# Eighteen weight sums on GpSimd instead of VectorE, a planner that counts instruction packets, and three held tiles released one by one

## The chip, the cores and the metric

One NeuronCore of a Trainium2 chip runs the whole program. Its engines work side by side, each through its own list of instructions in order: TensorE (PE; its weight loads are listed apart as PEld), VectorE (DVE), ScalarE (ACT), GpSimd (POOL) and SyncE (SP), which here only issues DMAs. They wait for each other through semaphores. The metric is the device time of one execution in microseconds, the median over the runs shown.

## The reference

Two steps, one behind the other, in float32 (the weights come as 64-bit floats, and the kernel turns them into 32-bit ones itself):

```python
# delta rule: 4 batches x 8 heads, 768 steps, head dimension 48
k_n = k / (norm(k) + 1e-6)
for t in range(768):
    y[t] = q[t] @ state
    state = state + beta[t] * outer(k_n[t], v[t] - k_n[t] @ state)
# then, on x = y as (3072 tokens, 384): RMS norm and a gated feed-forward network
xn = x / sqrt(mean(x*x) + 1e-6) * rms_g
out = (silu(xn @ w_gate) * (xn @ w_val)) @ w_out      # 384 -> 1536 -> 384
```

## The kernel before

The 768 steps are cut into 12 chunks of 64. Within a chunk the recurrence is a triangular system: products of keys (`scores`, `invert`), an inversion in small steps on VectorE (lines 709 to 807 for chunks 0 and 1, lines 869 to 930 for the later ones, with a round trip through DRAM), products with values and state (`recur`), the update of the state. Each chunk gives 256 tokens, on which the feed-forward network runs: for chunks 0 and 1 plainly (`ffn_plain`, up-products L1331, down-products L1313), for chunks 2 to 11 with fewer products by sums of factors (`ffn`, L1426, and `down`, L1483). So PE has two kinds of work: long streams of 128-row products, and bursts of small products (64 instructions or more in about 1 us) that carry the recurrence.

Every piece of work is an operation of a `Plan`: engine, estimated duration, what it reads and writes. The order of all 2790 operations is written out in the string `ORDER`. The text of the kernel does not search for it; it was found beforehand. At build time `Plan.times` walks this order and works out a start for each operation; from these starts follow which PSUM bank each result gets (there are eight) and where PE gets filler matmuls on an identity matrix (L1594), which go to a bank of their own and keep PE busy while the first chunk is prepared. `Plan.run` then emits the instructions. `OVERLAP`, `BEGIN`, `FETCH` and the like are constants of that estimate. In the version before, the supply of PE with instructions is estimated as a backlog that is filled by work and drained at a rate (`FETCH`, `AHEAD`).

The weights come in 18 pieces of 128 partitions by 768 values of 64 bits (`weights`). For each piece: one DMA of 768 KB into one of seven `raw` places, two ACT operations (L475 and L476) that take the upper and the lower 32-bit words, one DVE shift (L470), and one sum of the two words (L473) into `w_in` or `wo_sb`, from where the feed-forward network reads them. The seven `raw` places lie in tiles that are used otherwise later: three in `more`, two in `hf`, two in `wsum`. The first four pieces are loaded at once. The next three places are held back by `hold` (L493): a one-column POOL copy from `u_` into each place, so that the DMA of the piece has to wait for chunk 0's `u_`.

Names that return below: `norms` (L584 to L612) makes 1/norm(k) with a POOL power (L589, L608); `invert` and its steps L776 (transpose), L782 and L801 (small products), L795 and L807; `pt` (L633); `mr0` (L1134) and the L1114 products give u and y of a chunk; L1214, L1220 and L1221 make the RMS factor `rs`, the last two on POOL; L1232, L1236 and L1241 scale `yn` with it, L1259 transposes `yn` for the feed-forward network. L819 scales the keys on POOL. L1052 is the first product with the state.

Two functions carry the part that differs:

```python
P.add("DVE", 0.57, shifted, pr, w=cak)              # L470
P.add("DVE", 0.97, added, pr, r=cvk + cak, w=done)   # L473
def hold():
    for n in range(HELD, 7):
        t = raw[n].bitcast(FP32)[:, 0:1]
        P.add("POOL", 0.15, ..., 29, r=[("u", 0, 0)], w=[("raw", n)])
```

Of the kernel before, what the change touches and what calls it, by code (L numbers as in the profile page):

```python
# [9 lines left out]
FP32 = mybir.dt.float32  # L10
# [6 lines left out]
C = 64  # L17
W = 32
# [3 lines left out]
FETCH, AHEAD = 67.0, 120.0  # L22
EARLY, FETCH0, AHEAD0 = 130.0, 50.0, 150.0
# [9 lines left out]
    "#.#'#&#3#)#4###,#-#(#/#*#0#T#C#`#W#>#^#a#_#w#U#X#k#Y#$#Z#d#l#b#n#m#o#c#H#t#V#e#+#u#f#[#]#q#v#x#s#R#y#S#@#z#M#p#{#1#|"  # L33
    "#?#2#}#E#i#~#j$C$#${$$#r$'$($%$&$)$*#N$D$/#J$.#D$+$0$1$,$H#I%$$E#=$2$F$-%)#K$7$5#L$3$8$6$<#O#h#A$=$>$;$4$9#P$G$?%V$:"
    "#g$I$B#F$L$K$J$i$l$O$N$M#B$P$Q$R&2%Y$[$S$@#G$T$]%W%Z$^$V$k$j$U$_$v%X$f$q%e$`$a$W$m$b$Y%[$c$d#Q$X$Z$e$n$o&Q$A&E%]%`%^"
    "$|&F$p%a$~$w&I%_&G%b$x&H&J$y$s%3%c$r&M%d$g%.&K$t&N$h&3&L$z#5&R&O%f$}$u'2%g%+&4&P%h'3%%%#&S'4&+%i%&&,&T%j%*%=%k&X%8%l"
    "&U%/%B%,&Y&V(4%1%m(5&^%n&Z%0#8&_&-#7&[%q%G%r%o%2&W%4%s%p&]&`%x%5%6%y%L&.#:%t%z%C#<&/&a%{%u%7&0%v%-%D'-%w%}%~%|%'%(&c"
    "&#&1%:#%&5&d'Q%H'0%9&b&?%E%?%Q%F'T'a%J'R&''.%I'1&&&@%K&$&('S&7%;&)'U&%#6'/%>'V&*&e%@'5%A'W'X%<'8%R'Y&h':'[%T%S&f'Z'9"
    "(6&i']%U&8'7%M&6&m'6&j(7%N&g(8'^)-#9).(<'K(9&k):#;';);%O&r'<%P'_&s&9'=)/'?&n)0'>(:'L&l)n'M&o&t&p'b&u&q'@'`'N)q'A'c)o"
    "'B&:&w'P)r'd'e)p'O'f'C&v'g'h'G'i)s'j&x&A)u'k*P'H&|&C&y'l'D'E'F)t&{'m'I'J)y&z&})w'n&B)v'o'$&~*Q'#)x'p'%&D'q(;(I'r's'&"  # L40
    "'t)<(E){'*'''u(=(J'v(Q(F(K)1'w'x(>(G'y(H)K)2'z(L)z)=(M(C(?)>(N(@)L('(R()(O)}'{(P)?(%(W)~(*)M(+)|(X(,((*#($(S(A*$(D*%"
    "(T(&*&'~*''((Y(U*((#'}(V(-'|*)(Z)N&;(.***W(/*X*+(](2'+*,(1')(0)O(^(3*-)P)Q([*.(_&<)R*/(B*R(c(`)S(a(d*0*S(h(e*T*1)T*2"
    "*U*3&=*4(i(f*5)U)m(m*6(j(k(n)@*:*V*9)V(r,9*Y*8)X*7)W(s-$(o)Y(p*^)3,<(t,:)G(w,;)[*G)H(x,=*H*B)l*C,>)4*<(u*=)I+s*>,@*F"
    ",?(|)5)Z,C(y+u,B)A(},D)6,A(z*I)7*@)a*D)B(b*E)b)C,K*?)D*A)])c)E,L(g,F*;)^)_,E)d(l)`*J-#)e+t)f*K)8(q)g*M-+)9*L*O)h(~*`"
    "*Z)i*N)j',)#)k+y)F*[,G(v+z,H,I,J,M-%({,N+{,O,P,Q*b,R-&*d,S*c-',T)$*e,U-(,V)%,W)&,X*f)',Y*h)(*g*_)*-)+0,Z)+*j))*i.i-*"
    "*n*k),+2*o.j*p,[*t,]+v*u*q*l,^*v.l*r.k,_*z*a*w+w*s*x*{+4*m*y,`.m+3+(,a+x+5+8,b+$+),c+**|+%.n,d+<++*}+1,e+,*]*~+=+6,f"
    ")J+|,h,g+7,i+-+9.o+D+.+&+:+>+'+#+/,k+B+},t+~+_,s+?,$,r-,+C/V+@+E,8+F-2.p+H,m+G,l,#+J,w+I,v,%+N,7,j+K,n.q+O,q+L,p+A.H"
    "+P,u.r+Q.s+;+R+M,'+Z.w.~+V.v+S,&.t,,+T+W,x.u,-+U.E,o,y/U+X,z.G,(.F,|+a+Y.x,)+],.,/.y+g,},*&>,++`+[-0.I+e,~,0,{+^/^.J"
    ",1,2/#.K+h--,3,4,5+c,6/W.z+f.{.|.}/$/X+k/%/&+b/'/(-.+d/)-/-4/*+l-1/Y/+-6-5+n/,+m+i/Z-7/-.M/.-://-8+j/0-<-9/1+o/[/2-@"
    "-;1?+p-=+r-_+q-A->-B/31@-3-F-C-H/4-G-D-a-?-I/51B-L1A-c/]-M-J-E/6-b-V-d/71C-K-N-W-g/8-X-Y-R/9-`-O-k/:1D.L-e-S/;-l.N-T"  # L50
    "-P-f/>-U-h/<-Z1E.O/=.P-s-Q/?.R-[-m.Q-]-q.S-t-n/J.1/F1F.U/I.T-i.V-o-^-u.h/H-r-p/K/_1G-v/L/M.g-w1H-j1I-y.W-x1T1L-}.-1J"
    ".%1K-~1M/N.#.X.&.)/E-z2,.$0x-{.*.'/O-|1O/`.(.Y...2.+1N/P.,/D.3.//T/B.0/S0z/G1U/b/C/Q.9.7/R.Z.4/A/@.5.8.:2-/c0y1P/a1Q"
    ".=.61R.[1S1V1W.]1X.^0~1Y._1Z.>1[.@0{1]/e1#.`.?.;.a2..b.c.d.e.f2//g/f20/i.<1^1_/k21/j1`/h.A0|1a/l1b/m.B1c1$.D/o.C22/n"
    "/s3r/p/u/t/q/y/r3s/v/{3t1d/z/d/}/|1e0#/~1f0}3u1%/w230$1g240-1&1'053v1h1)4_0)1(0.071i1*0/0900/x1,1j3w060%1+0*0;0:1-1k"
    "084`0A1l0<0=1m0B3x0+010&1n0>0'0C1.021o0I0D031q0?0G0,1p1>0J040K1/0(0H3y1r0O0L0E1=0M0P1~3z1y0N0Q1{0R0S25103{3|0W3}3N0X"
    "3~0T4$260Y4#0Z0U0F4+2#0[0@1}0`2$0d0]110V1|0^4,1v0_0f3P4%0a1u1z0b0l1t2%1s0c0j1x122&1w0e4&0g1328142;152'3O160h172(182*"
    "192)1:2+0m0k3T1;0i1<274'0n3U4(4)4*4a4-4.0p4/40414b42430o2=0q4c440r2?450s4d2<2A462@470t2B2>48492C0u0v2I4e0w2D2E4g6H2J"
    "292h2F2j4:6I6J2O4;2K2P4<2Q2L6K2U4=2R4f2M3Q2G2N2V2S3R2H4>2`2T6L4?2k2l2:2a2[4@2b2m2p2c3S4A3V2W6M4B2i2t2X4C2n2]2Y4D2^3W"
# [18 lines left out]
    "?->o>m?/>p>n@0?)?.@1@2?%?*?3@4@3?+?1?0?4@5?2?,?9@6@7?=?:@8?E@9?>?5@:???;?@?G?6@<?F?A?&@;?I?H@=?B?7?K?<?J?C?M?L?Q?N?S"
    "?D@>?R?W?8?T?Y?X?[@??^?]?Z?d?U?_?O@@?`?e?h?f?a?l?g?b?i@A?t?V?j?c?k?m?P?v?n?p?u?o?r?q?z?w?s@B?x@C?}@D?{@E@F@G@$@H?y?|"
    "@I@J@K?~@%@L@&@'@M@#@O@N@Q@P@S@R@U@T@(@V@Y@)@*@`@Z@+@[@a@b@]@f@^@c@x@W@g@d@X@p@e@z@q@l@_@r@{@s@|@m@yA$@}@~@tA#A(A%@u"
    "A*A)@v@hA+A.A,@i@nA2@w@j@oA/@kA0A&A-A3A4A1A:A5A6A;A>A7ABA8A?A<AJA9A@A'A=AAACALAFADAKAEAHAGAOAMAIATANARAQAPAVASAUAXAW"  # L80
    "A]A^A_AYAZA["
# [34 lines left out]
class Plan:  # L116
# [38 lines left out]
    def times(self, order, banks, until):  # L155
# [8 lines left out]
        server, self.end, mode, backlog, lands = 0.0, 0.0, 0, 0.0, []  # L164
        for op in order:
# [41 lines left out]
    def run(self, free, filler=None, until=0.0):  # L207
# [24 lines left out]
def kernel(  # L232
# [209 lines left out]
    def weights(first, last):  # L442
# [14 lines left out]
        for n, (dst, src, keys) in list(enumerate(todo))[first:last]:  # L457
# [14 lines left out]
            def added(dst=dst.bitcast(U32), top=tiled(top), rest=tiled(rest)):  # L472
                nc.vector.tensor_tensor(out=dst, in0=top, in1=rest, op=ALU.add)  # L473
# [1156 lines left out]
```

## Time and profile before

| | |
|---|---|
| Median of 3 runs | 668.11 us (666.66, 668.11, 669.87) |
| The profiled execution | 668.94 us, of which 667.2 us from the first instruction to the last |
| PE busy, PEld busy | 654.4 us (98%), 604.8 us (91%) |
| DVE busy | 543.3 us (81%) |
| ACT, POOL busy | 295.7 us (44%), 133.7 us (20%) |
| PE instructions | 9934 matmuls and as many weight loads |
| DMA moved | 69.36 MB, 104 GB/s on average |

A busy PE in such a profile is not a PE without losses, as a matmul's span covers its whole passage. The chain of waits is of more use: it starts from the last instruction and goes back from each step to what released it. In it "issue" is time in which an engine waited for nothing that the profile shows. The windows view gives, for each engine in a stretch, busy time and in brackets the number of instructions; the timeline gives start, duration, engine, line, operation, tiles, shape and count, and at the end the idle time before it with what ended it.

### The profile page before, as it was taken

To read this page: it belongs to the slowest core of one execution; us is meant where nothing else is said; L and a number is where in the kernel's file an instruction comes from. 1 tells how busy PE (TensorE), PEld (TensorE's weight loads), DVE (VectorE), ACT (ScalarE), POOL (GpSimd) and SP (SyncE) were. 2 spreads that over 40 slices of the span, in tenths; PEclk is the share of its full clock that TensorE was granted. 3 is DMA by queue.
4 is the path that set the end of the run, shared out by engine and by line. 5 is a ranking of instruction groups with operands and counts; after the bars stand their busy time and mean duration, and the time that the engine had idled before them with its cause. 6 is when DMAs were issued, how large, how long until landed. Compare 5 with 4: busy or idle time off the path is not lost.

```text
span 667.2 us, 23209 instructions
## 1 busy us (share of the span) xinstructions
PE 654.4 (98%) x9934; PEld 604.8 (91%) x9934; DVE 543.3 (81%) x1147; ACT 295.7 (44%) x705; POOL 133.7 (20%) x204
## 2 busy tenths in 40 slices
PE   9999999999999999999999999999999999999997
PEld 5687887887799999999999999999999999999997
DVE  5879799888898798799888898799898799557463
ACT  4677553235336435454445345344445244263240
POOL 2210423021610410520410410420410301000000
PEclk9999899999999999999999999999999999999999
DMA  9959754666465566376375565666355333300101
GB/s 213 239 157 269 203 140 72 109 160 103 64 113 78 118 106 127 68 136 102 68 126 98 88 113 108 111 114 114 73 98 103 74 63 67 63 31 20 25 1 25
DMA packets 270423, 69.36 MB, mean 104 GB/s; under 512 B 257456, under 2 KB 262576, under 8 KB 270000
## 3 DMA queue, kind: packets, MB, share of 16 engines
q1 hardware_dynamic: 269280, 67.68, 51.1%
q8 instruction: 78, 1.28, 0.8%
q10 hardware_dynamic: 1040, 0.20, 0.2%
q14 instruction: 25, 0.20, 0.1%
HBM read 49.76 MB, written 22.02 MB: 108 GB/s over the span
## 4 chain that ended last, share of the span: by engine, by line
PE 91%; DVE 3%; issue 2%; POOL 2%; SPq 1%; DMA 1%; ACT 0%; POOLq 0%; ACTq 0%
PE bank L1426 40%; PE bank L1483 19%; PE bank L1331 8%; PE bank L1313 4%; PE bank L563 3%; PE bank L1037 3%; PE bank L1594 3%; PE bank L1114 2%; PE bank L1100 1%; PE bank L782 1%; PE bank L801 1%; PE bank L1171 1%; PE bank L979 1%; PE bank L999 1%; SPq L377 1%
## 5 line engine op out<-in xcount | busy, mean ns | idle before, releaser
L1426 PE MATMUL bank<-xf,w_in 128*128 128x128 f32 x1440 | 178.8, 276 | 0.3 <-DVE tmp L1436 0.3
L1426 PEld LDWEIGHTS bank<-xf,w_in 128*128 128x128 f32 x1440 | 169.3, 192 | 1.8 <-DVE tmp L1436 0.5
L1436 DVE TENSOR_TENSOR tmp<-tmp,bank 128x512 f32<-128x512 f32 x180 | 120.1, 682 | 46.9 <-PE bank L1426 28.9
L1426 PE MATMUL bank<-xf,more 128*128 128x128 f32 x960 | 122.8, 276 | 0.1
L1426 PEld LDWEIGHTS bank<-xf,more 128*128 128x128 f32 x960 | 114.9, 192 | 1.3 <-DVE tmp L1436 0.3
L1438 ACT COPY tmp<-bank 128x512 f32<-128x512 f32 x120 | 68.5, 587 | 99.9 <-PE bank L1426 78.5
L930 DVE TENSOR_REDUCE acc<-acc 128x30 f32<-128x90 f32 (+4 forms) x150 | 71.0, 473 | 5.2
L1442 ACT ACTIVATE tmp<-tmp 128x256 f32<-128x256 f32 x120 | 47.6, 415 | 61.9 <-DVE tmp L1436 61.8
L1483 PE MATMUL bank<-wo_sb,hf 128*128 128x192 f32 x360 | 64.0, 329 | 0.0
L1483 PEld LDWEIGHTS bank<-wo_sb,hf 128*128 128x128 f32 x360 | 58.0, 190 | 1.1 <-issue 0.4
L924 DVE TENSOR_TENSOR acc<-acc,at 128x60 f32<-128x60 f32 (+4 forms) x150 | 52.9, 353 | 5.9 <-POOL at L904 2.8
L1443 DVE TENSOR_TENSOR hf<-tmp 128x256 f32<-128x256 f32 x120 | 47.7, 418 | 3.0 <-ACT tmp L1442 2.2
L608 POOL TENSOR_TENSOR knrm<-ksum,half 128x16 f32<-128x16 f32 x11 | 32.0, 2913 | 85.2 <-DVE ksum L587 85.1
L869 POOL TENSOR_TENSOR at<-at,beta_b 128x256 f32<-128x256 f32 (+3 forms) x32 | 18.0, 593 | 149.0 <-DMA at<-dkk 149.0
L1313 PE MATMUL bank<-wo_sb,hf 128*128 128x384 f32 x96 | 33.8, 488 | 1.1 <-issue 1.1
L1331 PE MATMUL bank<-xp,w_in 128*128 128x256 f32 x144 | 34.7, 397 | 0.1
L1331 PE MATMUL bank<-xf,w_in 128*128 128x256 f32 x144 | 33.0, 382 | 0.0
L1331 PEld LDWEIGHTS bank<-xp,w_in 128*128 128x128 f32 x144 | 28.0, 198 | 4.5 <-DVE hf L1340 0.2
L1283 DVE TENSOR_TENSOR xf<-xf 128x256 f32<-128x256 f32 (+1 forms) x70 | 27.5, 432 | 5.2 <-ACT xf L1253 2.6
L1331 PEld LDWEIGHTS bank<-xf,w_in 128*128 128x128 f32 x144 | 26.9, 190 | 4.5
L950 POOL COPY acc<-acc 128x128 f32<-128x128 f32 x40 | 16.3, 438 | 71.4 <-DVE acc L930 70.7
L1313 PEld LDWEIGHTS bank<-wo_sb,hf 128*128 128x128 f32 x96 | 17.8, 190 | 10.3 <-issue 1.3
(207 smaller groups left out, 989.4 us busy)
## 6 DMA issues: line engine op xcount, KB each, us to landing
at<-dkk SPq DMA_DIRECT2D x20, 256.0 KB, 4.3
vt<-in_v_dram SPq DMA_DIRECT2D x24, 192.0 KB, 4.4
out_dram<-tmp SPq DMA_DIRECT2D x48, 96.0 KB, 2.2
k<-in_k_dram SPq DMA_DIRECT2D x23, 192.0 KB, 4.7
dks<-k SPq DMA_DIRECT2D x14, 256.0 KB, 4.0
kt<-dks SPq DMA_DIRECT2D x28, 128.0 KB, 3.8
more<-in_moe_w_gate_dram SPq DMA_DIRECT2D x4, 768.0 KB
more<-in_moe_w_out_dram SPq DMA_DIRECT2D x4, 768.0 KB
```

The costliest lines, as they stand in the source:

```text
L608: P.add("POOL", 2.95, lambda: nc.gpsimd.tensor_tensor(out=knrm[i2], in0=ksum[i2], in1=half, op=ALU.pow), pn, r=[("ksum", i2), "half"], w=[ ...
L924: nc.vector.tensor_tensor(out=acc[:, 1:3, 0:n, j + 2 : W].rearrange("p a i t -> p i a t"), in0=acc[:, old, 0:n, j : j + 2, None].to_broadc ...
L930: nc.vector.tensor_reduce(out=acc[:, new, 0:n, j + 2 : W], in_=acc[:, lo : lo + 3, 0:n, j + 2 : W].rearrange("p a i t -> p i t a"), axis=A ...
L1283: P.add("DVE", V(128 * n), lambda dst=dst, a=a, b_=b_, op=op: nc.vector.tensor_tensor(out=dst, in0=a, in1=b_, op=op), pxv, r=[("xp", 0), ( ...
L1313: nc.tensor.matmul(po[p].t[:, 0:DM], hf[:, spot(f), 128 * p : 128 * p + 128], wo_sb[:, spot(f)], start=(f == f0), stop=(f == f1 - 1), skip ...
L1331: nc.tensor.matmul(ps.t[:, TOK * side : TOK * side + TOK], w_in[:, side, h_, 3 * t + i_, n : n + 128], x_[:, 2 * t : 2 * t + 2].rearrange( ...
L1426: nc.tensor.matmul(g.t[:, 128 * z : 128 * z + 128], fac[:, side, 128 * f : 128 * f + 128], xf[:, xs], start=(begin and z == 0), stop=False ...
L1436: P.add("DVE", V(512), lambda t=t, g=g: nc.vector.tensor_tensor(out=t, in0=t, in1=g.t, op=ALU.add), -1, r=[g], w=[tk], last=g)
L1438: P.add("ACT", A(512), lambda t=t, g=g: nc.scalar.copy(t, g.t), -1, r=[g], w=[tk], last=g)
L1442: P.add("ACT", A(256), lambda t=t: nc.scalar.activation(out=t[:, 0:256], in_=t[:, 0:256], func=ACTF.Silu), -1, w=[tk])
L1443: P.add("DVE", V(256), lambda t=t, f0=f0, p=p: nc.vector.tensor_tensor(out=hf[:, spot(f0) : spot(f0) + 2, 128 * p : 128 * p + 128], in0=t[ ...
L1483: nc.tensor.matmul(g.t[:, 0:192], a_[:, f], b_[:, f], start=(begin and f == 0), stop=(f == 5), skip_group_check=True)
```

## The change

```diff
-FETCH, AHEAD = 67.0, 120.0
-EARLY, FETCH0, AHEAD0 = 130.0, 50.0, 150.0
+PACKET = (130.2, 254.45, 314.0)
+LAG = (4.2, 0.55, 7.0)
...
 ORDER = (
...
 # Plan.times
+        first, each, reach = PACKET
+        count, asked, used, there, pe = 0, 0, 0, {}, 0.0
+        lag = lambda t: LAG[0] + LAG[1] * min(max(server - t, 0.0), LAG[2])
...
-                rate, store = (FETCH, AHEAD) if s > EARLY else (FETCH0, AHEAD0)
-                fill = 6.0 if s < until else 0.0
-                backlog = max(0.0, backlog - (rate - fill) * (s - at["PE"])) + op.size - rate * op.dur
-                late = max(0.0, backlog - store) / rate
-                backlog, end = max(0.0, backlog - rate * late), end + late
+                op.fill = []
+                if s < until and any(x == SPARE and s < SPARE or x <= pe for x in free):
+                    op.fill = fillers(pe, s)
+                pe = s + op.dur
+                count += 4 * len(op.fill)
+                while first + each * asked <= count:
+                    there[asked] = s + lag(s)
+                    asked += 1
+                more, late, long = count + op.size, 0.0, end - s
+                while True:
+                    a, b = first + each * asked, first + each * used + reach
+                    if a >= more and b >= more:
+                        break
+                    if a <= b:
+                        t = s + late + (long * (a - count) / op.size if op.size else 0.0)
+                        there[asked] = t + lag(t)
+                        asked += 1
+                    else:
+                        t = s + late + (long * (b - count) / op.size if b > count else 0.0)
+                        if used < asked and there[used] > t:
+                            late += there[used] - t
+                        used += 1
+                count, end = more, end + late
...
 # weights
             def added(dst=dst.bitcast(U32), top=tiled(top), rest=tiled(rest)):
-                nc.vector.tensor_tensor(out=dst, in0=top, in1=rest, op=ALU.add)
+                nc.gpsimd.tensor_tensor(out=dst, in0=top, in1=rest, op=ALU.add)
...
-            P.add("DVE", 0.97, added, pr, r=cvk + cak, w=done)
+            P.add("POOL", 1.55, added, pr, r=cvk + cak, w=done)
...
     def hold():
-        for n in range(HELD, 7):
-            t = raw[n].bitcast(FP32)[:, 0:1]
-            P.add("POOL", 0.15, lambda t=t: nc.gpsimd.tensor_copy(out=t, in_=u_[:, 0, 0:1]), 29, r=[("u", 0, 0)], w=[("raw", n)])
+        for n, t, key in ((HELD, u_[:, 0], ("u", 0, 0)), (HELD + 1, ms[0][:, 0], ("ms", 0, 0)), (HELD + 2, xp1[:, 0], ("x1", 0))):
+            out_, in_ = raw[n].bitcast(FP32)[:, 0:1], t[:, 0:1]
+            P.add("POOL", 0.15, lambda out_=out_, in_=in_: nc.gpsimd.tensor_copy(out=out_, in_=in_), 29, r=[key], w=[("raw", n)])
```

There are three parts and a consequence. The 18 sums (L473 before, L494 after) move from DVE to POOL. `Plan.times` counts PE's instructions: it takes it that they come in packets of 254.45, that a packet is asked for at instruction 130.2 and then every 254.45, is needed 314 instructions after that, and is there 4.2 us after the request plus up to 3.85 us more by the load of the DMA queue. The three held places are released one after the other: by chunk 0's `u_`, by its mean square `ms`, and by its normalised and transposed rows `xp1`. The consequence is a new `ORDER`: all 2790 operations are the same but for the engine of the sums, and 333 of the 580 PE operations stand at another place in PE's list than before; the lists of the other engines and of the DMAs differ as well. PE's filler matmuls go from 26 to 24 instructions. Line numbers behind line 200 rise by 21.

More of the change, by code (lines that the diff above doesn't have):

```diff
@@ L37 @@
[L37 to L46, printed above, removed]
@@ L77 @@
[L77 to L81, printed above, removed]
+    "#.#'#-#w###4#(#)#*#3#0#/#>#`#W#C#^#a#T#_#,#k#X#&#Y#Z#b#l#d#n#m#o#e#t#U#H#c#V#1#u#f#+#[#]#r#v#x#q#y#s#z#j#p#{#S#|#D#i"
@@ new lines @@
+    "#}#R#I#~#M$#$$$%$&$'$(#$$)$*#E#g$/#J$+%$$.$C#2$,$1#K#?$0$D#L$2#N$-$6#@$3$E$5$F$;$7${#A#h#=$<$8#F#P$9$>$H#O$=$:$?$G%V"
+    "$I$B$L$K$J$4$i#G$l$O$N$M$P$Q$R%Y$[$S$f$T$]%Z$^$j$V$_$q$U$W#B%)$`$a%W$X$Y$b%X$@$d$c#Q$Z%[$e$m$n$k%e&Q$v&E%]&3$o%^%`$r"
+    "&F$p$s&I%a%_%.&G$t$g&2&J%b$A#5&H$h$u%c%%&R$w%d$x&M%f%&%3$y'2&K#;%g%*%=%h&N$|&L$z#%&S&O%+$~&P&T'3%i$}&+%j&W&,&U%#'4%B"
+    "&V&X%8%k%0#<&Y%,%/%l%G%1&^%m&-%n%2&_&Z&[%r%-&]&.%5%p&4%'%4%o&/%x&`%(%y%L%C(4&c%z&0#6%q%:%6#:%E%9&d%s%>%Q&a%t&e%7%{%u"
+    "&6%v%D%|&1&&%H&''Q%w'-%F%~'.'0'R%J%I&b%}&#%@(<&(&5%K'a'T(5&)'U#7'S'/&$#8&*%?#9'1'V&7&%&f%A'8'W'X'5%;%S%<'Y&h%R'6']'["
@@ new lines @@
+    "(6)-&m'Z%T%N(;%U'7&i':(7'b'9'O%M&g).'^&j&8(8):'K)/(9%O';)0&k&l'<'_&n%P&r&o(:&9'M)n&p&q'='L'>'P&s'`'?'@'c&w&t&?'d&u)o"
+    "&@&:'e&x'f)p'B'g)q'h'G&|'H'i&y'A'I'j&}'J)r'k&C)K*P'l)s'm&v)u&z)t'n'C&~&{)y'o'D'E&A'F)x'p'$*Q'q)v'%)w'r&B'#(E's&D't(F"
+    ")1'u){'&'v(G(H(I'N);'*'y)<'w(J)2'x(='z(M(K)z)M)L(N(L)=(*)>(>'|(O''(&(S'{(@)}(,(+(P(?(T(C)3('(()|(X(U(#)~'((V(Q(Y',*#"
+    "()(%(R*$($(Z*%'~*&(A(^*'*X*((-'}*))N(.**(/(B([(W&;*+(0(1*W(3*,)O(_(D(2*-)Q(`(a(c*.*/*R(d)S*0&<(h)R*S(i*T*1(]*2(j*U)P"
+    "*3(e)T(f*4)4*5)?(m)U*6(k-$(n*V*9)m,9(r*Y*7(o*8(p(s*:)l)V)G,:(t,<,;(w(u,=*D)5)W*=)H(x*<)X*E)Y*G,>*H*@)Z+s*C,?*;,@(|+u"
@@ L82 @@
+    "?y@K@L?|@M@%@'@O@&?~@P@N@Q@#@S@R@U@T@(@V@Y@)@+@`@Z@*@[@a@W@b@]@f@^@c@d@g@x@e@p@l@q@z@_@r@m@|@s@{@X@y@t@}@~@uA$@vA#@n"
+    "A(@w@oA%A*A)@hA+A.@iA2@jA,@kA/A0A-A3A4A&A1A:A5A6A;A>A<A7ABA8A?AJA'A@A9AAA=ACALADAKAEAFAGAOAHAIATANAMAPARAQAVASAUAXAW"
+    "A]A_A^AYAZA["
 )
@@ L163, in times @@
                 g.taken, g.uses = False, g.left
-        server, self.end, mode, backlog, lands = 0.0, 0.0, 0, 0.0, []
+        server, self.end, mode, lands = 0.0, 0.0, 0, []
+        first, each, reach = PACKET
+        count, asked, used, there, pe = 0, 0, 0, {}, 0.0
+        lag = lambda t: LAG[0] + LAG[1] * min(max(server - t, 0.0), LAG[2])
         for op in order:
@@ L216, in run @@
                 spare = [x for x in free if x[0] == SPARE and s < SPARE or x[0] <= pe]
-                if s < until and spare:
-                    filler(fillers(pe, s), spare[-1][1])
+                if op.fill:
+                    filler(op.fill, spare[-1][1])
                 pe = s + op.dur
```

69 lines of the change are left out of this document (35 added, 34 removed).

## The prediction

> **What bounds the kernel now.** I read the page first, then the chain of waits, then windows and timelines where the chain leaves PE's stream.
>
> ```profile
> PE 654.4 (98%) x9934; PEld 604.8 (91%) x9934; DVE 543.3 (81%) x1147; ACT 295.7 (44%) x705; POOL 133.7 (20%) x204
> ...
> q8 instruction: 78, 1.28, 0.8%
> ...
> PE 91%; DVE 3%; issue 2%; POOL 2%; SPq 1%; DMA 1%; ACT 0%; POOLq 0%; ACTq 0%
> ```
>
> PE bounds the kernel, and 91% of the chain is its own matmuls, which the change leaves alone. Only 9% of 667.2 us, some 60 us, can be argued about, a part of it before PE's first feed-forward matmul. The chain there and behind it (start, us, what):
>
> ```profile
> 13.58 1.09 PE bank L563 x64
> ...
> 28.33 0.81 PE bank L782 x26
> 29.14 0.63 issue
> ...
> 30.77 1.05 PE bank L782 x32
> ...
> 32.45 1.99 PE bank L801 x64
> ...
> 37.57 0.86 DVE w_in L473
> ...
> 43.40 0.93 issue
> ...
> 44.60 7.98 PE bank L1331 x36
> ...
> 71.08 1.31 issue
> ...
> 73.87 4.43 PE bank L1331 x12
> ...
> 122.86 2.79 PE bank L1331 x12
> ...
> 171.18 1.06 issue
> ```
>
> Two things cost time. A weight sum (L473) is itself a link of the chain at 37.57. And PE stops four times here for 0.63 to 1.31 us with nothing to wait for. The windows view, from the start to these stops and to one of 0.9 us at 265.4 (L999, below), counts the instructions that PE had begun (in brackets, PE and PEld):
>
> ```profile
> 0.00:29.20 29.20, 27.72 (x350) 18.24 (x350) 20.76 (x64) 16.18 (x40) 6.19 (x11) 1.00 0.93 218
> 0.00:43.40 43.40, 40.62 (x731) 29.65 (x731) 29.73 (x86) 23.79 (x62) 11.59 (x19) 1.00 0.82 208
> 0.00:71.30 71.30, 67.28 (x1113) 52.03 (x1114) 55.89 (x146) 44.22 (x98) 14.50 (x20) 1.00 0.84 213
> 0.00:171.25 171.25, 165.39 (x2636) 131.17 (x2637) 143.27 (x323) 87.68 (x202) 39.22 (x47) 0.99 0.72 167
> 0.00:265.40 265.40, 258.55 (x4165) 219.58 (x4165) 223.80 (x491) 129.51 (x301) 62.28 (x84) 0.99 0.65 142
> ```
>
> The sums are 700, 1462, 2227, 5273 and 8330. From the first they are 3.0, 6.0, 18.0 and 30.0 steps of 254.5. PE's 19868 instructions over 78 packets of the instruction queue give 254.7. So PE stops where a packet of its own instructions is not there yet. The new planner's constants put these places at 444.2 + 254.45 k: 698.7 for k = 1, as measured.
>
> The Trainium skill speaks against that reading. "Runtime: NRT & Kernel Launch", section Instruction fetch mechanics, says that instructions come in 16 KiB blocks of 256, which fits the packets here, but also that the fetch is mostly hidden since instructions are issued more slowly than they are filled in. The second half doesn't hold in this trace, which has stops of up to 1.31 us; by it the sum below would be 2.1 us and not 7.1.
>
> **The change part by part.** *Sums off DVE.* DVE loses 18 instructions of 0.95 us (six of them in the first row below, the others at 946 to 960 ns), 17.2 us between 28 and 96 us. POOL gains 18. The trace has no integer sum on POOL; the nearest row is L819, two inputs of 768 elements, 1.48 us, so 26.6 us in all. A bound above is twice that row, 2.95 us, if integers cost it more; below is L1062's rate, 0.84 us for 384 elements, which gives 1.68 for 768 and so no gain over L819.
>
> ```profile
> L473 DVE CUSTOM_DVE_ANT_0 w_in<-xf,tmp x6: 948/954/1076, 28.7 to 85.3; 128x1536 uint16<-128x1536 uint16 x6
> L819 POOL TENSOR_TENSOR k<-k,krec 128x768 f32<-128x768 f32 x11 | 16.2, 1477 | 31.8 <-issue 14.3 <-DVE krec L612 11.0 <-PE bank L1331 4.5
> L1062 POOL TENSOR_TENSOR r<-r,bt x2: 836/836/837, 76.3 to 79.0; 128x384 f32<-128x384 f32 x2
> 28.72 0.95 DVE L473 CUSTOM_DVE_ANT_0 w_in<-xf,tmp 128x1536 uint16<-128x1536 uint16 x1
> 29.59 0.44 DVE L776 STREAM_TRANSPOSE x2bd<-mt 128x256 f32<-128x256 f32 x1
> 29.95 0.65 DVE L633 TENSOR_TENSOR pt<-bank,mask_p 128x512 f32<-128x512 f32 x1
> 30.70 1.01 PEld L782 LDWEIGHTS bank<-mt,m1bd 64*64 64x64 f32 x32 [0.17 <-DVE pt L633]
> 20.00:40.00 20.00, 18.91 (x419) 15.58 (x417) 16.40 (x40) 10.73 (x29) 5.98 (x7) 1.00 0.74 191
> 40.00:60.00 20.00, 18.71 (x320) 15.98 (x320) 16.78 (x41) 16.45 (x31) 1.17 (x4) 1.00 0.81 213
> 60.00:80.00 20.00, 18.69 (x273) 15.44 (x272) 17.51 (x38) 12.46 (x20) 7.39 (x6) 0.91 0.86 240
> 80.00:100.00 20.00, 19.89 (x405) 16.82 (x404) 17.59 (x33) 10.95 (x26) 4.76 (x3) 1.00 0.60 163
> ```
>
> Off the chain this buys nothing: from 45 us on PE has its stream. On the chain it counts twice. At 28.72 a sum stands ahead of the transpose L776 and of `pt` L633, for whose bank PE's second L782 block waits until 30.70: 0.95. At 37.57 it is a link: 0.86. Together -1.8 us. The bounds are 0 (the power on POOL or the L801 products take over) and -3.1 (the whole detour from 28.33 to 32.45 but for one L782 block of 1.05, since the new list puts the q transposes L540 ahead of both L782 blocks). I take -1.8, as both pieces are seen. On POOL a wait is added: each sum waits for ACT and the shift, and behind it in POOL's list stand the power, the key scaling L819 and `rs`. In the new list one sum stands ahead of chunk 0's first `rs`, between it and the release by `u_`, and the next two stand behind the second `rs`. So `rs` is cleared unless that one sum is late.
>
> One sentence of the skill on the price: "GPSIMD Engine Reference", section 3.1, has a two-input sum of 2048 elements at 4497 ns, by which 768 would take an estimated 1.69 us and POOL's load would be 3.8 us more, off the chain but for one sum of 0.2.
>
> *Packets.* I walked both built lists of PE with the cadences of the rows (64 products of 64 columns 1.09, 32 of L782 1.05, 12 of L1331 2.79) and looked at the 314 instructions ahead of each packet's place. In the old list they last under 5.5 us at 10 places, in the new one at 3; behind the first feed-forward matmul at 8 and at 1. At 71.08 the stretch grows from 4.4 to 7.2 us, at 43.40 from 4.6 to 6.1, at 265.4 from 3.7 to 6.3. At 29.14 it stays (5.7 and 5.8), at 171.18 it doesn't grow (6.9 and 6.3), and the place between 29 and 43 with 4.9 us falls to 4.0.
> - Before 45 us: 0.93 goes, up to 0.9 may come at the shortened place; -0.5, bounds +0.9 and -1.56 (both stops).
> - 71.08: -1.31. Behind it PE ran at half clock for some 3.6 us (granted 0.91 in 60:80, so 20 x 0.09 / 0.5): 12 matmuls of L1331 took 4.43 instead of 2.79. That goes with the stop: -1.64. If the stop stays, both stay.
> - 171.18: 0, bounds -1.06 and +0.6.
> - Behind 180 us, the waits of PEld:
>
> ```profile
> PEld bank L999 <- issue: 2.1, 5, 0.9
> PEld bank L1483 <- issue: 1.2, 6, 0.2
> ...
> PEld bank L1100 <- issue: 0.7, 3, 0.2
> PEld bank L979 <- issue: 0.5, 2, 0.2
> 103.08 0.62 PE L1259 MATMUL bank<-ident,yn 128*128 128x128 f32 x3 [0.57 <-ACT yn L1241]
> ```
>
> L1483's six of 0.2 look like a change of shape and stay. Of L999, L1100 and L979 (3.3 together) and what stretches without an idle row I take -2.0, bounds 0 and -4.0.
>
> *The three releases and the new DMA order.* The third held piece now waits for chunk 0's transposed rows, and on SP a load into `more`, which went out at 27.41, stands behind two releases.
>
> ```profile
> 27.41 1.31 SPq L377 DMA_DIRECT2D more<-in_moe_w_gate_dram  x1
> ...
> 39.95 0.57 SPq L377 DMA_DIRECT2D wsum<-in_moe_w_val_dram  x1
> ```
>
> That load feeds the second half of the network, which PE's list reaches after all up-products of the first, and the last release comes about when the old `wsum` load went out, so I take 0. If that cover is gone, the third piece's columns wait: one down- and two up-products (some 1.3 and 2.79) are 4 us of other work on PE, beyond which each us counts.
>
> *Other places.* At 103.08 PE waits 0.57 for `yn`, behind POOL; -0.3, bounds -0.57 and +1.6. A list packed more tightly meets small delays that were in gaps before: +0.5, bound +5.
>
> Sum: -1.8 -0.5 -1.31 -1.64 -2.0 -0.3 +0.5 = -7.05. The profiled execution took 668.94, so 661.9; the median lies 0.83 below it: 661.1, called 661.0.
>
> **The rivals.**
> 1. *The stops don't go*: the DMA load, not the spacing, decides when a packet lands, and the new list has stops at other places. For: 171.18 stopped with a 6.9 us stretch. Left are the sums (-1.8) and 103.08 (-0.3): 668.11 - 2.1 = 666.0. The skill's rule that fetches are hidden gives the same time. Against: five stops at whole packets.
> 2. *POOL and DVE get in each other's way* (slower). The one mechanism: a POOL sum holds off a DVE instruction with two SBUF inputs, or the reverse. For:
>
> ```profile
> 99.29 1.33 DVE L869 TENSOR_TENSOR at<-at,beta_b 128x1024 f32<-128x1024 f32 x1
> L1220 POOL TENSOR_SCALAR ms<-ms x11: 218/222/1082, 99.6 to 593.9; 128x2 f32<-128x2 f32 x11
> ```
>
> A 222 ns step took 1082 while L869 ran. Six sums stand on POOL beside chunk 1's inversion. If all 18 block fully, DVE gains 17.2 and loses 26.6: 9.4 us more in 20:100, where it has 68.3 of 80 busy already, so chunk 1 and PE end 9.4 late, against 4.75 saved (1.31, 1.64, 1.8): 668.11 + 4.7 = 672.8. It decides from 0.83 of the sums' time on, where 26.6 f - 17.2 reaches 4.75. Against: L470 and the products from PSUM have one SBUF input.
> 3. *All of it works*: sums -3.1, early stops -1.56, late -4.0, with -1.31, -1.64 and -0.3 as above and no new delay: 668.94 - 0.83 - 11.91 = 656.2.
>
> **How the numbers follow.** Forecast 0.66, rival 1 0.12, rival 2 0.08, rival 3 0.14. The range 656.0 to 667.0 holds rivals 1 and 3; left out are rival 2 and some 0.1 at the ends. The forecast's own range is 657.5 to 665. Within 0.5% (about what a measurement tells from no change) is 664.8 to 671.4. Faster: 0.63 of the forecast, rival 3, a quarter of rival 1: 0.80. Same: 0.12. Slower: rival 2, 0.08.
>
> **What would show it.** First feed-forward matmul near 42 us (44.60 before); no "issue" of 1 us and no half clock at 70 to 77 us; POOL's sums at 1.5 us each; fewer waits of L999 behind 180 us. Sums over 2.5 us on POOL, a DVE step beside them stretched by 1 us, or PE idle for `rs` or for a weight between 45 and 105 us would make it wrong.

## The result, and the profile after

The changed kernel takes 664.47 us (median of 6 runs, 661.92 to 666.53), the kernel before beside it 668.08: a ratio of 0.994, 95% interval 0.991 to 0.997. A second batch of 12 runs on another chip gave 662.79 against 667.45, 0.9935 (0.991 to 0.996). So 3.6 to 4.7 us went, where 7.0 were forecast. The profiled execution took 664.82 us, its span 663.1 against 667.2. Lines behind line 200 stand 21 further on in the new file: L473 is now L494, L470 L491, L1331 L1352.

The page of the changed kernel: busy times, then the shares of the chain of waits.

```profile
PE 650.8 (98%) x9930; PEld 602.4 (91%) x9930; DVE 539.4 (81%) x1129; ACT 296.8 (45%) x705; POOL 167.5 (25%) x222
...
PE 89%; DMA 4%; DVE 3%; ACT 1%; issue 1%; POOL 1%; SPq 1%; ACTq 0%; POOLq 0%; DVEq 0%
```

DVE lost 18 instructions of 0.95 us, 17.2 us, and yet its busy time fell by only 3.9. POOL rose by 33.8, not by 26.6. "issue" on the chain is down from 2% to 1%, and in its place stands DMA with 4%: it runs over loads of `vt`, `wsum` and k (7.83, 7.34 and 9.70 us, begun at 24.38, 42.49 and 54.02).

The windows of the changed kernel (columns as before: stretch, busy us and instructions of PE, PEld, DVE, ACT, POOL, granted clock, DMA share, GB/s):

```profile
20.00:40.00 20.00, 18.56 (x478) 15.71 (x477) 14.46 (x37) 11.59 (x27) 10.59 (x9) 1.00 0.60 173
40.00:60.00 20.00, 18.63 (x205) 15.26 (x205) 17.47 (x35) 17.31 (x30) 10.38 (x9) 1.00 1.02 275
60.00:80.00 20.00, 19.17 (x407) 16.37 (x406) 16.18 (x34) 13.14 (x23) 15.73 (x9) 1.00 0.84 230
```

In 60:80 the clock is 1.00 where it was 0.91: the half clock behind the old stop is gone. In 40:60, which was to be a closed stream of matmuls, PE is still idle for 1.4 us. What it waits for (engine, line, what for, us in all, times, longest):

```profile
PE bank L1334 <- POOL w_in L494: 1.4, 1, 1.4
PE bank L1155 <- DVE mt L828: 1.0, 1, 1.0
PE bank L1058 <- issue: 0.9, 1, 0.9
PE bank L803 <- ACT mt L789: 0.8, 1, 0.8
PE bank L1121 <- ACT tmp L1463: 0.6, 1, 0.6
PE bank L1155 <- issue: 0.6, 1, 0.6
...
PE bank L1447 <- ACT tmp L1459: 0.4, 1, 0.4
```

Two stops at packets are left, at 82.4 (0.6, after 2732 instructions, k = 8.99) and at 371 us (0.9, k = 44.97), where there were five (k is the number of the packet, by 444.2 + 254.45 k as in the prediction). But four new waits for other engines stand beside them, and the first is behind a sum on POOL. The timeline around it (start, duration, engine, instruction):

```profile
42.46 5.45 PE L1352 MATMUL bank<-xp,w_in 128*128 128x256 f32 x24
...
44.02 1.83 POOL L494 TENSOR_TENSOR wo_sb<-xf,tmp 128x768 uint32<-128x768 uint32 x1 [0.88 <-ACT tmp L497]
44.37 1.89 DVE L715 SCALAR_TENSOR_TENSOR acc<-m1bd,side,acc 128x128 f32<-128x128 f32 x2
46.18 0.55 DVE L491 TENSOR_SCALAR more<-more 128x768 uint32<-128x768 uint32 x1
46.65 2.19 DVE L715 SCALAR_TENSOR_TENSOR acc<-m1bd,side,acc 128x128 f32<-128x128 f32 x2
46.87 1.82 POOL L494 TENSOR_TENSOR w_in<-more 128x768 uint32<-128x768 uint32 x1 [1.02 <-DVE more L491]
48.76 0.41 DVE L1361 TENSOR_TENSOR hf<-tmp,bank 128x256 f32<-128x256 f32 x1
...
49.27 1.21 PE L1334 MATMUL bank<-wo_sb,hf 128*128 128x384 f32 x3 [1.37 <-POOL w_in L494]
```

The first feed-forward matmul comes at 42.46 (44.60 before), as forecast. Then L715 on DVE, 0.35 us an instruction before, takes 1.89 and 2.19 for a pair, and each pair ends 0.2 to 0.4 us behind a sum on POOL; `hf` (L1361) stands behind them on DVE, and PE needs `hf`. The name that the profile gives, POOL's L494, had ended at 48.69; the last to come was `hf`, at 49.17. The same groups of DVE between 20 and 110 us, in the kernel before and in the changed one (count, busy us, mean ns, idle before):

```profile
L694 DVE SCALAR_TENSOR_TENSOR acc<-m1bd,side,acc 128x128 f32<-128x128 f32 x4 | 1.1, 347 | 0.0
L587 DVE TENSOR_SCALAR ksum<-ksum 128x16 f32<-128x16 f32 x3 | 0.5, 169 | 0.0
```

```profile
L491 DVE TENSOR_SCALAR more<-more 128x768 uint32<-128x768 uint32 x5 | 4.3, 855 | 0.0
L715 DVE SCALAR_TENSOR_TENSOR acc<-m1bd,side,acc 128x128 f32<-128x128 f32 x4 | 4.1, 1058 | 0.0
L608 DVE TENSOR_SCALAR ksum<-ksum 128x16 f32<-128x16 f32 x3 | 2.7, 898 | 0.0
```

L694 and L715 are one line, L587 and L608 another. Over all lines that both kernels have, the same DVE instructions took 13.6 us longer in 20:110 (each line's mean after less its mean before, times its count; below, "the stretch on DVE").

### The profile page after: what moved, and what is told of

Its sections match the earlier page's. It is cut to its first block, busy times and chain, and to the rows that moved or that the text cites. A ratio compares the mean times of both kernels' runs of the same rounds, so it can differ in the third digit from the quotient of the medians.

```text
span 663.1 us, 23217 instructions
## 1 busy us (share of the span) xinstructions
PE 650.8 (98%) x9930; PEld 602.4 (91%) x9930; DVE 539.4 (81%) x1129; ACT 296.8 (45%) x705; POOL 167.5 (25%) x222
## 4 chain that ended last, share of the span: by engine, by line
PE 89%; DMA 4%; DVE 3%; ACT 1%; issue 1%; POOL 1%; SPq 1%; ACTq 0%; POOLq 0%; DVEq 0%
PE bank L1447 40%; PE bank L1504 21%; PE bank L1352 7%; PE bank L1334 4%; PE bank L584 3%; PE bank L1058 3%; PE bank L1135 2%; PE bank L1121 2%; DMA k<-in_k_dram 1%; DMA vt<-in_v_dram 1%; PE bank L1192 1%; DMA wsum<-in_moe_w_val_dram 1%; PE bank L1000 1%; PE bank L1020 1%; SPq L398 1%
## 5 line engine op out<-in xcount | busy, mean ns | idle before, releaser
L1447 PE MATMUL bank<-xf,w_in 128*128 128x128 f32 x1440 | 178.4, 276 | 0.4 <-ACT tmp L1459 0.4
L1447 PEld LDWEIGHTS bank<-xf,w_in 128*128 128x128 f32 x1440 | 169.3, 192 | 2.2 <-ACT tmp L1459 0.6
L1447 PE MATMUL bank<-xf,more 128*128 128x128 f32 x960 | 122.5, 276 | 0.0
L1447 PEld LDWEIGHTS bank<-xf,more 128*128 128x128 f32 x960 | 114.8, 192 | 0.8 <-issue 0.2
L951 DVE TENSOR_REDUCE acc<-acc 128x30 f32<-128x90 f32 (+4 forms) x150 | 70.9, 473 | 5.2
L1504 PEld LDWEIGHTS bank<-wo_sb,hf 128*128 128x128 f32 x360 | 58.0, 190 | 0.9
L890 POOL TENSOR_TENSOR at<-at,beta_b 128x256 f32<-128x256 f32 (+3 forms) x32 | 19.6, 643 | 139.2 <-DMA at<-dkk 139.2
L1334 PE MATMUL bank<-wo_sb,hf 128*128 128x384 f32 x96 | 34.5, 492 | 1.4 <-POOL w_in L494 1.4
L1352 PE MATMUL bank<-xp,w_in 128*128 128x256 f32 x144 | 33.1, 382 | 0.0
L1352 PE MATMUL bank<-xf,w_in 128*128 128x256 f32 x144 | 33.0, 382 | 0.0
L1352 PEld LDWEIGHTS bank<-xf,w_in 128*128 128x128 f32 x144 | 27.0, 190 | 4.5
L1352 PEld LDWEIGHTS bank<-xp,w_in 128*128 128x128 f32 x144 | 26.9, 190 | 4.5
L1241 POOL TENSOR_SCALAR ms<-ms 128x2 f32<-128x2 f32 x11 | 2.7, 245 | 102.0 <-ACT bank L1229 101.9
```

The costliest lines, as they stand in the source:

```text
L951: nc.vector.tensor_reduce(out=acc[:, new, 0:n, j + 2 : W], in_=acc[:, lo : lo + 3, 0:n, j + 2 : W].rearrange("p a i t -> p i t a"), axis=A ...
L1334: nc.tensor.matmul(po[p].t[:, 0:DM], hf[:, spot(f), 128 * p : 128 * p + 128], wo_sb[:, spot(f)], start=(f == f0), stop=(f == f1 - 1), skip ...
L1352: nc.tensor.matmul(ps.t[:, TOK * side : TOK * side + TOK], w_in[:, side, h_, 3 * t + i_, n : n + 128], x_[:, 2 * t : 2 * t + 2].rearrange( ...
L1447: nc.tensor.matmul(g.t[:, 128 * z : 128 * z + 128], fac[:, side, 128 * f : 128 * f + 128], xf[:, xs], start=(begin and z == 0), stop=False ...
L1504: nc.tensor.matmul(g.t[:, 0:192], a_[:, f], b_[:, f], start=(begin and f == 0), stop=(f == 5), skip_group_check=True)
```

## The experiments

The theory from here: A, the packets and the new order carry the gain, and the move of the sums gives back by contention what it takes off DVE. Rival B: taking the sums off DVE is itself worth the 1.8 us of the prediction. Each experiment's ratio is to the kernel before on the same chip.

**1. The new order with the sums on DVE.**

```diff
 # the changed kernel
-                nc.gpsimd.tensor_tensor(out=dst, in0=top, in1=rest, op=ALU.add)
+                nc.vector.tensor_tensor(out=dst, in0=top, in1=rest, op=ALU.add)
```

> The changed kernel with its new order and planner, but the 18 weight sums back on DVE (the planner still counts them on POOL, so the lists of PE, ACT and SP are the same). Theory A (the packets and the order carry the gain; the move of the sums gave back by contention what it took off DVE): the other DVE instructions lose the stretch of 13.6 us that they have in the changed kernel, the 18 sums of 0.95 us come back, and the time is within 1.5 us of the changed kernel's 664.5 (663.0 to 666.0); PE's wait of 1.37 us at 49.27 for hf shrinks below 0.7. Rival B (taking the sums off DVE is itself worth the 1.8 us that the prediction put on it): 666.3 or more, with PE's waits for DVE longer before 45 us. In both the stops at the old packet places stay away.

Measured: 663.34 us, ratio 0.993 (0.990 to 0.996). The stretch on DVE is 0.4 us instead of 13.6. Its waits of PE, and its group of L608:

```profile
PE bank L1121 <- ACT tmp L1463: 1.0, 1, 1.0
PE bank L1058 <- issue: 0.9, 1, 0.9
PE bank L803 <- ACT mt L789: 0.9, 1, 0.9
PE bank L822 <- DVE kk L816: 0.5, 1, 0.5
PE bank L1155 <- DVE mt L828: 0.5, 1, 0.5
```

```profile
L608 DVE TENSOR_SCALAR ksum<-ksum 128x16 f32<-128x16 f32 x3 | 0.5, 156 | 0.0
```

The wait of L1334 for `hf` is gone, and the whole gain is there without the sums on POOL. B falls.

**2. The old order with the sums on POOL**: the reverse edit, one line, in the kernel before.

> The kernel before with its old order and planner, only the 18 weight sums on POOL. Theory A: DVE's other instructions are stretched by 10 us or more between 20 and 110 us, POOL's sums take 1.8 us each, PE's stops at 28.9, 43.2, 70.9, 171.1 and 265.3 us stay (they move with the time only), and the time is 667 to 671, so no gain of the size of the sums' term. Rival B (the relief of DVE is the gain): 666.3 or less with the stops still there. Rival C (POOL and DVE block each other fully): 672 or more.

Measured: 670.76 us, ratio 1.005 (1.002 to 1.007): the move alone makes it slower. Time and stretch (12.6 us) came as A has it. The stops didn't all stay, which A had expected: in this profile only the one near 171 us did (0.5 at 173.8), the one near 71 shrank to 0.2, and those at 28.9, 43.2 and 265.3 are gone. Ahead of the one at 43.2 PE now waits for data (1.4 at 40.9); ahead of the first and the last it doesn't, and why they stayed away is open. So the 3.3 us are what is left after the stops that went. Its waits of PE, and DVE's timeline ahead of the first of them:

```profile
PE bank L1331 <- DVE hf L1340: 1.8, 1, 1.8
PE bank L1134 <- POOL r L1062: 1.5, 1, 1.5
PE bank L1171 <- DVE yn L1232: 1.4, 1, 1.4
```

```profile
52.43 1.92 DVE L728 TENSOR_TENSOR at<-at 128x128 f32<-128x128 f32 x1
54.27 1.81 DVE L729 COPY acc<-at 128x16 f32<-128x16 f32 x1
```

L729 copies 16 columns; in the kernel before it took 0.18 us and L728 0.40. Here both last as long as the sum on POOL beside them, and `hf` comes 1.8 late.

**3. and 5. Packets moved in the old order.** Tiny matmuls in place of warming ones add 116 instructions to PE's stream near 15 us. The edit of the fifth; the third had 30 of them for one warming matmul:

```diff
 # the kernel before
     def filler(n, warm):
+        if len(n) > 8:
+            n = n[5:]
+            for _ in range(34):
+                nc.tensor.matmul(warm[0:64, 0:64], ident[0:64, 0:64], ident[0:64, 0:64])
         for w_ in n:
```

> The kernel before, with one of PE's warming matmuls in its idle time near 15 us replaced by 30 tiny ones, which take the same time but add 116 instructions to PE's stream; nothing else changes. Packet theory: every later packet place falls 116 instructions earlier. The stops at 70.9 (1.31, with the half clock behind it), 171.1 and 265.3 us vanish; by the walk of PE's list with the rows' cadences new short stretches are at k = 37 (4.2 us) and k = 44 (5.0 us), that is near 310 and 363 us, with stops of about 1 us each. Time 664 to 666 (668.1 - 1.31 - 1.64 - 1.06 - 0.9 + 1.9 = 665.1). Rival (the stops belong to the instructions or to the moment at which they occur: a transfer, an engine that is late): they stay where they are and the time is 668.1 within 0.7.

Measured: 668.45 us, 1.003 (1.001 to 1.006). The stops at 70.9, 171.1 and 265.3 were gone, but the tiny matmuls had a price of their own (their row, and that of 64 products L563 ahead of them):

```profile
13.39 1.16 PE L563 MATMUL bank<-qt,kt 64*64 64x64 f32 x64
14.37 3.66 PE L1596 MATMUL bank<-ident 64*64 64x64 f32 x60
```

One after the other on one tile they took 61 ns each, not L563's 18, so PE began its inversion (L782) at 26.11 us, 2.45 late. Hence the fifth:

> The third experiment again without its side effect. There the 30 tiny matmuls took 3.66 us and not the 0.9 of the one warming matmul that they replaced, so that the first feed of the inversion (L782) began 2.45 us late. Here 34 tiny ones stand for five warming matmuls (4.2 for 4.5 us), again 116 instructions more in PE's stream. Packet theory: L782 begins within 0.6 us of the kernel before (23.66), the stops at 70.9, 171.1 and 265.3 us and the half clock behind the first are gone as in the third experiment (3.2, 1.0 and 0.75 us between equal places of PE's work there), some 1.5 us of new waits near 80 us stay: 3 to 4 us less than the kernel before, 663.5 to 665. Rival (the time does not hang on the places; the third experiment was slower for its own reasons): 667.5 within 0.7.

Measured: 665.61 us, 0.999 (0.995 to 1.002). L782 began at 24.08; the three stops are gone, and no stop of 0.6 us at a packet is left in the profile, nor did one of that size come at k = 37 or 44. The medians are 1.8 us apart, half of what was expected, but the interval holds 1, so that a gain isn't shown. In the profiled execution PE runs into the next waits, and into half clock behind them (the waits, then windows of the fifth kernel):

```profile
PE bank L1331 <- ACT xp L1268: 1.5, 1, 1.5
PE bank L801 <- ACT kk L793: 1.5, 1, 1.5
...
PE bank L801 <- DVE r L1059: 1.1, 1, 1.1
```

```profile
80.00:85.00 5.00, 3.51 (x102) 3.40 (x100) 2.92 (x6) 3.74 (x7) 0.08 (x1) 0.67 0.69 237
85.00:90.00 5.00, 5.00 (x86) 4.82 (x79) 2.84 (x6) 3.06 (x6) 0.00 (x0) 0.65 0.36 58
```

The stop at 71 us had covered chunk 1's inversion, which was late as well: with the stop away, L801 waits 1.1 and 1.5 us for DVE and ACT between 78 and 82. In the same way the first row stands where the stop at 43 us was: the first feed-forward matmul, L1331, waits there for `xp` and begins at 43.94, 0.6 us earlier than before. In all PE waits 6.3 us for other engines behind 15 us in this profile and 1.8 in that of the kernel before. But it is a profile of one of the slowest executions of this kernel (669.47 us, of 663.3 to 671.6), with a mean granted clock of 0.995; the two fastest, 663.3 and 663.6, had 0.999 and 1.0, so that the half clock at least isn't in each of them.

**4. Packets moved in the new order**: 23 tiny matmuls for one warming one, 88 instructions more.

> The changed kernel, with one of PE's warming matmuls in its idle time near 15 us replaced by 23 tiny ones, which take the same time but add 88 instructions to PE's stream; nothing else changes, and the planner isn't told. Packet theory: the planner chose this order for packet places that now lie 88 instructions off; by the walk the stretches ahead of k = 8 (4.1 us, near 73 us), 26 (2.7), 31 (4.9), 37 (4.2), 44 (3.5) and 57 (3.0) become short, so that five or six new stops of 0.8 to 2 us appear and the two old ones (82 and 371 us) go: 668 to 671. Rival (the new order gains by other means, the places don't matter): 664.5 within 0.7.

Measured: 668.53 us, ratio 1.001 (0.999 to 1.004): the whole gain is lost. The tiny matmuls' own price is up to 1.4 us of that (L803 began at 24.15 instead of 22.71); with it taken off, 2.6 to 4.3 us remain, by which batch of the changed kernel one takes (664.47 or 662.79, both on other chips). PE's stops at packets are 5.0 us in its profile, against 1.5 in the changed kernel's. The windows from the start to three of its new stops, and the first of these in the timeline:

```profile
0.00:75.60 75.60, 72.16 (x1240) 57.43 (x1240) 56.69 (x143) 49.39 (x104) 37.74 (x34) 1.00 0.88 230
0.00:220.10 220.10, 215.14 (x3528) 177.82 (x3528) 182.76 (x396) 110.50 (x258) 84.06 (x85) 0.99 0.66 149
...
0.00:426.50 426.50, 419.25 (x6833) 375.49 (x6834) 359.74 (x763) 202.83 (x480) 134.74 (x167) 1.00 0.62 127
```

```profile
77.22 0.54 PE L803 MATMUL bank<-mt,m1bd 64*64 64x32 f32 x12 [1.52 <-issue]
```

The instructions begun there are 2480, 7056 and 13667: k = 8.00, 25.98 and 51.97. PE stops where a packet begins, whatever instruction stands there. The walk by stretches named k = 8, 26 and 44 rightly (44 with a stop of 1.0 at 364 us) and missed 48 and 52; at 31, 37 and 57 nothing came. So each of the stops lies at a place that the count gives, but which of the places stop depends on more than the stretch ahead.

**6. and 8. The changed kernel again, and the release by `u`.** In the eighth all three held places are released by the first write of `u`:

```diff
-        for n, t, key in ((HELD, u_[:, 0], ("u", 0, 0)), (HELD + 1, ms[0][:, 0], ("ms", 0, 0)), (HELD + 2, xp1[:, 0], ("x1", 0))):
+        for n, t, key in ((HELD + i, u_[:, 0], ("u", 0, 0)) for i in range(3)):
```

> The changed kernel once more, to stand beside the next two on one chip. Both theories: 663.5 to 665.5, ratio to the kernel before 0.994 within 0.003.

> The changed kernel, but all three held places of the weights are released by the first write of u, as before; order, planner and sums as in the changed kernel. The prediction put the staged release at 0: then the time is that of the changed kernel within 0.7 us. Rival (the staged release starts loads at a better time and earns a part of the gain): 1.5 us or more above the changed kernel, with the first loads into the held places going out earlier and another transfer (k or vt) later.

Measured: 662.79 us, 0.9935 (0.991 to 0.996), and 662.09 us, 0.992 (0.990 to 0.995), on one chip. The staged release earns nothing. In this second profile of the changed kernel the first feed-forward matmul comes at 41.21 us, and in the first experiment, with the sums on DVE, at 41.25: the sums don't move it (the second profile of the changed kernel, then the first experiment):

```profile
41.21 5.45 PE L1352 MATMUL bank<-xp,w_in 128*128 128x256 f32 x24
```

```profile
41.25 5.45 PE L1352 MATMUL bank<-xp,w_in 128*128 128x256 f32 x24
```

**7. and 11. Entries of the order moved, sums on DVE.** The second load of `vt` goes ahead of a load that waits for ACT, the copies L789 ahead of the squares L605 that wait for a k load, `mt` L782 ahead of their reduction. The eleventh has the release by `u` besides.

```diff
 # Plan.run of the first experiment's kernel
         self.times(order, [t for t, _ in free], until if filler else 0.0)
+        for a, b, gap in ((15, 183, 0), (258, 260, 1), (283, 258, 1), (257, 284, 0)):
+            op = order.pop(order.index(self.ops[a]))
+            order.insert(order.index(self.ops[b]) + gap, op)
```

> The changed kernel with the 18 sums on DVE and four entries of the written order moved: the second load of vt on SP ahead of the load into more that stands behind ACT; ACT's two copies L789 of chunk 1 ahead of the squares L605 that wait for the k load; DVE's mt L782 ahead of the reduction of those squares. PE's list is the same. If the two waits of PE that these cause in the profile with the sums on DVE (0.5 to 0.7 us at 31.5 for mt L828, 0.9 to 1.1 us at 63.1 for mt L789) are on the path: 1.2 to 1.8 us less than with the sums on DVE alone, 661.5 to 662.5, and both waits gone. Rival (the next wait takes their place): 663.3 within 0.7 with the lost time at another place before 90 us.

> The seventh kernel (sums on DVE, four entries moved) with the release of all three places by u. If the 0.7 us of the release by u is real and adds to the rest: 660.7 within 0.7, ratio to the kernel before 0.990 to 0.992. If it was noise: 661.4 within 0.7.

Measured: the seventh 661.40 us, 0.992 (0.990 to 0.995), both waits gone from its profile. In their place stand two packet stops in L1158 (L1155, three lines on), at 33.1 and 79.6 us, k = 2.0 and 9.0:

```profile
PE bank L1158 <- issue: 0.9, 2, 0.5
```

The eleventh, on a third chip, 665.42 us against 668.54, 0.9955 (0.992 to 0.999), with 1.9 us of such waits in its profile. Between the two, nothing says that one of these versions beats the changed kernel: the seventh's interval overlaps that of the sixth beside it.

**9. and 10. The price of a sum, and its parts.** A single time each: the sums as additions of 32-bit floats (`top` and `rest` read as such), and each sum in four.

```diff
 # the tenth
-                nc.gpsimd.tensor_tensor(out=dst, in0=top, in1=rest, op=ALU.add)
+                h = dst.shape[2] // 4
+                for z in range(4):
+                    cut = lambda t: t[:, :, z * h : z * h + h]
+                    nc.gpsimd.tensor_tensor(out=cut(dst), in0=cut(top), in1=cut(rest), op=ALU.add)
```

> The changed kernel, but the 18 sums on POOL add the two words as 32-bit floats instead of integers, so the lowest bits of the weights are lost. It asks what made the sum's price 1.82 us where the prediction took 1.48 from L819. If the type does it: 1.5 us or less each, and the time 1 us or so below the changed kernel's. If three tensors of full size (L819 has its output in place and a factor repeated along the row) or the layout do it: 1.8 us each, time as the changed kernel's (662 to 666).

> The changed kernel, each sum on POOL cut into four of 192 columns. If DVE is held off for one whole instruction of POOL and goes next: the longest delay of a DVE step beside the sums falls from about 1.6 to 0.5 us and the stretch between 20 and 110 us from 13.6 to below 8 us; the sums themselves together cost 2.0 to 2.6 us (four starts for one), so the time is within 2 us of the changed kernel's. If POOL keeps what they share from one instruction to the next: the stretch stays at 12 us or more and single DVE steps still take 1.5 us longer.

Measured: 662.59 and 665.11 us. The sums by line in the changed kernel, the ninth and the tenth (duration min/median/max in ns, first and last start), and two of the tenth's groups on DVE (lines 3 further on):

```profile
L494 POOL TENSOR_TENSOR w_in<-xf,tmp x6: 1812/1826/1835, 25.9 to 83.7; 128x768 uint32<-128x768 uint32 x6
```

```profile
L494 POOL TENSOR_TENSOR w_in<-xf,tmp x6: 1812/1822/1835, 25.3 to 82.7; 128x768 f32<-128x768 f32 x6
```

```profile
L497 POOL TENSOR_TENSOR w_in<-xf,tmp x24: 582/596/909, 25.7 to 85.2; 128x192 uint32<-128x192 uint32 x24
```

```profile
L718 DVE SCALAR_TENSOR_TENSOR acc<-m1bd,side,acc 128x128 f32<-128x128 f32 x4 | 2.2, 595 | 0.0
L611 DVE TENSOR_SCALAR ksum<-ksum 128x16 f32<-128x16 f32 x3 | 1.5, 486 | 0.0
```

The type is not what makes the price. Cut in four, a sum holds a small DVE step off for one quarter: L611 takes 0.49 us on average and not 0.90 (0.65 at most), L718 0.60 and not 1.06, and the stretch on DVE is 8.0 us, just at the bound that was expected. So DVE goes next when the instruction on POOL ends. PE's time shows no gain from it, as the tenth has other waits, and from a single time no verdict on the whole follows.

## Why the prediction was right or wrong

*Direction and range held; the gain is half to two thirds of the forecast.* By the time alone 3.6 to 4.7 us lie about midway between the forecast's 7.05 and the 2.1 of rival 1; what decides between them is that the old stops went. One of the prediction's own signs of being wrong came: DVE steps beside a sum took over 1 us longer, and PE's 1.4 us at 49 came of that. At equal amounts of PE's own work (each matmul counted with its kind's cadence) the changed kernel's first profile was ahead by 2.1 us at the first feed-forward matmul, by 3.0 at 108 us, 4.1 at 212 and 4.2 at the end. The forecast's terms for these stretches were 2.3, 3.25, 0 and 2.0, less 0.5 for delays. These are figures of one execution each; in the second profile the first feed-forward matmul comes 1.25 us earlier than in the first.

- *Sums off DVE, -1.8: the step that failed.* The first feed-forward matmul is as early as forecast, but with the sums on DVE as well (41.25 us, and 41.21 with them on POOL), and in the old order moving them left it nearly where it was (44.25 us; 44.53 before, by the same view). So that this part of the forecast came out is luck: another cause stood in for the term. It is the new order and the two stops that went with it; which move of the order does it wasn't tried, and in the fifth experiment, with the stops gone in the old order, 0.6 us came of them. That a sum was a link of the chain at 37.57 said that its place was wrong, not its engine. The first experiment puts the term at 0 within the measurement, the second at +3.3 in the old order.
- *The sum's price, 1.48 us from L819:* it took 1.82, 32.8 us in all. L819 was the wrong row to lean on; the type is excluded, and what sets the two apart (three separate tensors of full size, a factor repeated along the row in L819) wasn't tried. The Trainium skill's estimate from "GPSIMD Engine Reference", section 3.1, 1.69, was the nearer one.
- *Rival 2, the contention:* its mechanism is real and its size was between. Of POOL's 32.8 us, 13.6 appear as delay on DVE, 0.41, below the 0.83 from which it was to decide. The sentence against it, that L470 has one SBUF input, was wrong: single instructions of that line took up to 2.09 us beside a sum. The prediction didn't weigh the rule that speaks against the change: the Trainium skill, "SBUF — State Buffer", section Who interferes with whom, has `tensor_scalar` and copies among the instructions that can take both of DVE's ports, and the one that starts first keeps the shared pair for its whole instruction. The runs agree: 16 columns took 1.8 us beside a sum of 1.8, and half a microsecond beside a quarter. Instructions that read PSUM (L1361, 0.41 us) kept their time, as did reductions (L606, 0.94 us, 0.93 before), which that section excludes as well.
- *Packets:* right as the cause of the stops. The fourth experiment moved the places by 88 instructions and took the gain away; the fifth moved the old ones and the old stops went. The DMA packets of the instruction queue, 78 of 16 KB in each trace, show it directly: counted from 0, packet k had landed 1.2 to 1.4 us before PE went on behind the stops at k = 1, 4, 7 and 19 of the kernel before (2.1 at k = 31), 1.2 and 1.4 us before it at k = 9 and 45 of the changed one, and 1.3 to 1.5 us at the five of the fourth experiment. The rule of the Trainium skill, "Runtime: NRT & Kernel Launch", section Instruction fetch mechanics, that fetching is mostly hidden, doesn't hold for PE in this kernel. So rival 1's main point, that the stops don't go, is out; that the DMA load has a say in when a packet lands wasn't tried. How much of the gain is the stops' own isn't shown either, as removing them in the old order gave none clear of noise.
- *71.08, -1.31 and -1.64:* stop and half clock are gone, as forecast, but some 1.8 us of the 3 arrived. The fifth experiment's profile shows a reason in the old order: behind the stop other waits were covered. The new order keeps one of these, L803 for `mt`, 0.8: ACT's copies stood behind the squares of a k load that took 9.70 us from 54.02. The half clock is also not in every execution of the kernel before: 15 of the 35 beside the sixth experiment have a mean granted clock of 0.999 or more, the profiled one 0.997, so that -1.64 was too much for the median.
- *171.18, 0: mis-sized.* The walk had the stretch ahead of this place no longer than before (6.9 and 6.3 us), and yet the stop of 1.06 went; the 1.1 us between 108 and 212 us above are of its size. Why this packet came in time is open.
- *Behind 180 us, -2.0: mis-sized.* Five "issue" waits of L999 were taken as packets; one of 0.9 was, three of the rest are 0.2 each and one, off the places of packets, 0.5. Such waits of 0.2 are still there, with a new packet stop at 371 us (PEld's waits there, changed kernel):

```profile
PEld bank L1058 <- issue: 1.7, 4, 1.0
PEld bank L1020 <- issue: 1.6, 7, 0.2
```

  Some 0.1 us came of it.
- *New delays, +0.5: mis-sized.* The new waits for other engines listed above, L1334, L1155, L803, L1121 and L1447, are 4.2 us. As some old ones went, PE's waits for other engines behind 15 us rose from 1.8 to 4.7 us, while its stops at packets and small "issue" waits fell from 5.0 to 1.5. Only the first goes with the sums on POOL; L1155 and L803 go with the order of SP and ACT, as the seventh experiment shows.
- *L1259, -0.3, and the releases, 0:* the wait for `yn` is gone from the list (0.57 before); the release by `u` made no difference clear of noise.

## What to carry to other kernels

Before a stream of instructions is moved to POOL to relieve DVE, list what DVE runs beside it: a copy, a scalar operation or a two-input instruction on SBUF can be held off for a whole POOL instruction, as up to 1.6 us here, and it is the small ones in a chain that cost, not the sum of busy time. A stop at an instruction packet is found by counting instructions, and proven by adding some ahead of it; removing it pays only as far as the next late engine. When an order is made anew together with an edit, run the old order with the edit and the new order without it before one gives the edit the credit.

## What the runs showed of the hardware that was not expected

- A DVE step of 16 columns took 1.80 us instead of 0.17 beside a sum on POOL of 1.82.
- Tiny 64x64 matmuls, one after the other on one tile, took 61 ns each, where the products of L563, spread over tiles and banks, took 18.
- PE went on 1.2 to 1.5 us after the DMA packet with its next instructions had landed, at all but one of the stops of 0.4 us or more in the profiles of the kernel before, the changed kernel and the fourth experiment.
- Half clock followed waits for data as well as packet stops: in the fifth experiment's profile the granted clock is 0.67 and 0.65 in the ten microseconds behind two waits of 1.1 and 1.5 us.
